# Where softmax and memory sums are divided out in a two-layer attention and Fourier kernel: through DRAM, or with 32x32 block transposes on VectorE

## The chip, the cores and the metric

The kernel runs on one core of a Trainium2 chip. The core has five engines that each work through their own list of instructions in the order written, and meet at semaphores: TensorE (PE; its weight loads are shown apart as PEld), VectorE (DVE), ScalarE (ACT), GpSimd (POOL) and SyncE (SP). SP computes nothing here; it issues every DMA, from one queue. Matmuls write to PSUM, eight tiles of 128x512 fp32; everything else is in SBUF or DRAM.

The metric is the device time of one execution in microseconds, as the median of several runs.

## What is computed

Two layers, each an attention with a compressive memory followed by a Fourier mixing. Cut to what matters:

```
S, D, H, Dh, N = 2048, 512, 32, 16, 4;  L = S // N          # four segments of 512 tokens
def A(x):                                                    # attention, segment by segment
    q, k, v = heads(x @ wq), heads(x @ wk), heads(x @ wv)
    g = sigmoid(beta);  M = 0;  z = 0                        # one gate for each head
    for s in range(N):
        a_dot = softmax(q[s] @ k[s].T * Dh**-0.5 + causal_mask) @ v[s]
        a_mem = (phi(q[s]) @ M) / (phi(q[s]) @ z + 1e-6)
        out[s] = g * a_mem + (1 - g) * a_dot
        M += phi(k[s]).T @ v[s];  z += sum(phi(k[s]))
    return out @ wo
def B(x):                                                    # real part of a 2-D DFT
    return Cr @ (x @ Wr.T) - Ci @ (x @ Wi.T)
for layer in range(2):
    x = x + A(layernorm(x))
    x = x + B(layernorm(x))
```

Both a_dot and a_mem are quotients: for every head and token a sum of weighted values over a sum of weights.

## The kernel before

**Units and tiles.** The 32 heads are four groups of eight, and a group is four pairs of heads. A unit `i` is one group in one segment of one layer, so there are 2 x 4 x 4 = 32 units. The value tile `vt` holds, for each pair, 16 value columns of the first head, 16 columns of ones, and 16 value columns of the second head. A matmul with 32 of these columns gives the weighted values of a head and its sum in one go: the two results of a unit, `e` and `o`, are PSUM tiles with tokens along the 512 columns, and in each block of 32 partitions (one head pair) 16 rows of values and 16 equal rows with the sum, values first in `e`, sum first in `o`. The same holds for the memory (`macc` in place of `vt`).

**The merge** (`t_merge`) makes one tile `n` out of `e` and `o`: values of the first heads from `e`, of the second heads from `o`, each divided by its sum and multiplied by its gate. It runs 56 times: 32 times for the softmax part (`gi` = 1, called by `s_m`), and 24 times for the memory part (`gi` = 0, called by `s_mem`; the first segment of a layer has no memory). ACT copies `e` and `o` whole to SBUF (`d`), makes the first half of `n` with a gate factor (`gm`) that is zero on the second heads' rows, and DVE adds the second half. Then four steps pass through DRAM, since a sum has to reach 16 partitions: one row of sums for each head is stored (`den`, two DMAs), loaded again with 128 partitions of 32 numbers (`dc`), inverted by DVE, stored (`rec`), and loaded with each row repeated over 16 partitions (`z`). One multiply on DVE or POOL ends the merge. `s_m` then adds the memory part and splits the result into two fp16 halves `ot`, which the output projection (`s_o`) takes once four units of a segment are done.

**What sets the order.** There are no loops over hardware iterations: the program is written out by a planner (`Plan`). Every part of the work is a Python generator that yields an engine, the tiles that it reads and the buffers that it wants; at each step the planner takes the part that can start first by its own model of the engines' times, and the instruction is appended to its engine's list. So a part with other operations, other costs or fewer waits changes the order of everything after it, on all engines. `tt` puts an elementwise operation of two tensors on DVE or POOL, whichever its model says ends it first. Buffers come from pools with a cap for each kind: all of `md`, `mz`, `en` and `ot` are kinds of 52 SBUF tiles `w`, `av`, `pj`, `ss` and `dft` kinds of the eight PSUM tiles `b`. The profile names tiles by these pool names, so most tiles read `w` or `b`; all instructions have the line of the helper `call` (L249).

**What else runs.** The attention's score matmuls run twice: `s_x` with queries along partitions, where DVE finds the row maxima (`t_max`: `junk` and `mx`), and `s_st` with keys along partitions, where ACT takes the exponential and POOL cuts the triangle (`t_sel`). `s_av` multiplies with `vt`. `s_c` prepares the DFT matrix for the first layer: a maximum over each block (`cam`, on DVE), a scale from it by way of PE, and a split into fp16 halves by ACT and POOL. `s_f` runs the DFT matmuls, `t_y` adds their results.

Of the kernel before, what the change touches and what calls it, by code (L numbers as in the profile page):

```python
# [8 lines left out]
F32 = mybir.dt.float32  # L9
# [3 lines left out]
AF = mybir.ActivationFunctionType  # L13
# [242 lines left out]
def body(ctx: ExitStack, tc: tile.TileContext, x, wq, wk, wv, wo, beta, wd, cs, out):  # L256
# [31 lines left out]
        xi0.append(xi)  # L288
    wsrc = [w.rearrange("(t p) n -> p t n", p=128) for w in (wq, wk, wv)]
    stage = [[y[:, 4 * n + g, :].rearrange("p (t n) -> p t n", t=KT) for n in range(3)] for g in range(NG)]  # L290
    gb = const.tile([128, 2, NG], F32, name="gb")

    def load(g, n):
        Y.dma_start(stage[g][n], wsrc[n][:, :, 128 * g:128 * g + 128])
# [17 lines left out]
    V.tensor_scalar(identf, jp, 0.0, None, op0=OP.is_equal)  # L312
    cmask = const.tile([128, 512], BF16, name="cmask")
    bd = const.tile([128, 2, 4, 32], F32, name="bd")
    gm = const.tile([128, 2, 2, NG], F32, name="gm")
    m0, m1, rp, ra = (const.tile([128, 1], F32, name=n) for n in ("m0", "m1", "rp", "ra"))
    done = set()
    ywritten = set()
    uses = {}
# [6 lines left out]
    def need(eng, *reads, tag=(), mode="m"):  # L326
        return eng, reads, (tag,) if isinstance(tag, str) else tag, mode
# [72 lines left out]
    def s_w():  # L400
        def part(n, g, how):
            i = 2 * g + n if n < 2 else 8
            yield need("A", tag="wv" if n == 2 else "wt")
            w = sb("wv" if n == 2 else "wt", F16, (128, 2, KT, 128))
            yield from how(w, stage[g][n], scl[:, i:i + 1])
            yield need("Y", w)
            Y.dma_start(wqkv[g][n], w)
            wnow[n, g] = w
            done.add(("W", n, g))

        def factors(g):
            for f, n, e in ((f_q, 0, -10), (f_k, 1, -10), (f_k2, 1, 12)):
                V.tensor_scalar(f[g], inv[:, 2 * g + n:2 * g + n + 1], 2.0 ** e, None, op0=OP.mult)
            V.tensor_scalar(f_s[g], inv[:, 2 * g:2 * g + 1], inv[:, 2 * g + 1:2 * g + 2], 2.0 ** 22,
                            op0=OP.mult, op1=OP.mult)

        for g in range(2):
            for n in range(2):
                yield need("V", stage[g][n])
                absmax(2 * g + n, flat(stage[g][n]))  # L420
        yield from scales(0, 4)
        for n in range(2):
            yield from part(n, 0, split)
        factors(0)
        factors(1)
        for n in range(2):
            yield from part(n, 1, split2)
        yield gate(*[("L", 0, t) for t in range(TT)])
        for g in range(NG):
            load(g, 2)  # L430
        for g in range(2, NG):
            for n in range(2):
                load(g, n)
        Y.dma_start(gb[:, 0, :], beta)
        for g in range(NG):
            yield need("V", stage[g][2])
            V.tensor_reduce(vm[:, g:g + 1], flat(stage[g][2]), axis=AX.X, op=OP.max, apply_absolute_value=True)
        V.tensor_reduce(amax[:, 8:9], vm, axis=AX.X, op=OP.max)
        for g in range(2, NG):
            for n in range(2):  # L440
                yield need("V", stage[g][n])
                absmax(2 * g + n, flat(stage[g][n]))
        yield from scales(4, 9)
        done.add("WL")
        factors(2)
        factors(3)
        for x in ((2, 0), (0, 2), (1, 2), (2, 1), (2, 2), (0, 3), (1, 3), (2, 3)):
            yield from part(*x, split2)
# [28 lines left out]
    def s_k():  # L477
        def bits(f, mask, scale):
            t = work.tile([128, 1], I32, name="bits", bufs=2)
            V.tensor_scalar(t, pi, mask, None, op0=OP.bitwise_and)  # L480
            V.tensor_copy(f, t)
            V.tensor_scalar(f, f, scale, None, op0=OP.mult)

        for i in range(NR):
            for t, c in ((qst[i], 0.0), (kst[i], K8192)):
                for a in range(2):
                    r = slice(64 * a + 32, 64 * a + 64)
                    yield need("G")
                    G.memset(t[r].rearrange("r p n -> r (p n)").bitcast(F32), c)
            done.add(("QI", i))  # L490
            done.add(("KI", i))
            if i == 0:
                yield need("V")
                V.memset(cmask[:, :384], 0.0)
                V.tensor_scalar(cmask[:, 384:], jp, 0.0, NEG, op0=OP.is_gt, op1=OP.mult)
                done.add("CM")
                yield gate(*[("L", 0, t) for t in range(TT)])
                for j in range(NR):
                    V.memset(vt[j][:, :, :, 1, :], 1.0)
                done.add("VI")  # L500
        yield need("V")
        bits(m1, 16, 1.0 / 16)
        V.tensor_scalar(m0, m1, -1.0, 1.0, op0=OP.mult, op1=OP.add)
        bits(rp, 3, 1.0)
        bits(ra, 64, 1.0 / 64)
        cj = sb("en", F32, (128, 2, 4, 32))
        G.iota(cj, pattern=[[0, 2], [1, 4], [0, 32]], base=0, channel_multiplier=0,
               allow_small_or_imprecise_dtypes=True)
        ca = sb("pn", F32, (128, 2, 4, 32))
        G.iota(ca, pattern=[[1, 2], [0, 4], [0, 32]], base=0, channel_multiplier=0,  # L510
               allow_small_or_imprecise_dtypes=True)
        yield need("V", cj, ca)
        V.tensor_scalar(cj, cj, rp, None, op0=OP.is_equal)
        V.tensor_scalar(ca, ca, ra, None, op0=OP.is_equal)
        V.tensor_tensor(bd, cj, ca, op=OP.mult)
        pl.close(cj, ca)
        yield gate("WL")
        yield need("A", gb)
        A.activation(gb[:, 1, :], gb[:, 0, :], AF.Exp, scale=1.0)
        A.activation(gb[:, 0, :], gb[:, 0, :], AF.Exp, scale=-1.0)  # L520
        yield need("V", gb)
        V.tensor_scalar(gb, gb, 1.0, None, op0=OP.add)
        V.reciprocal(gb, gb)
        for i in range(2):
            for j, m in enumerate((m0, m1)):
                V.tensor_scalar(gm[:, i, j, :], gb[:, i, :], m, None, op0=OP.mult)
        done.add("GM")

    def t_ln(src, xi, dst, key):
# [43 lines left out]

    def t_merge(e, o, gi, g, n, key):
        yield gate("GM")
        yield need("A", e, o, gm, tag=("md", "md"))
        ds = []
        for src in (e, o):
            d = sb("md")
            A.activation(d, src, AF.Copy)  # L580
            ds.append(d)
        A.activation(n, e, AF.Copy, scale=gm[:, gi, 0, g:g + 1])
        yield need("V", n)
        V.scalar_tensor_tensor(n, o, gm[:, gi, 1, g:g + 1], n, op0=OP.mult, op1=OP.add)
        pl.close(e, o)
        yield need("Y", *ds)
        den = tc.dram_tile([NP, 2, 512], F32)
        rec = tc.dram_tile([NP, 2, 512], F32)
        for a, d in enumerate(ds):
            Y.dma_start(den[:, a, :], d[16 - 16 * a:128:32, :], est=(530, 500))  # L590
        pl.close(*ds)
        yield need("Y", den)
        c = rg("dc", 3, F32, (128, 32))
        Y.dma_start(c, den.rearrange("p a (x c) -> (p a x) c", c=32), est=(350, 750))
        yield need("V", c)
        if not gi:
            V.tensor_scalar(c, c, 1e-6, None, op0=OP.add)
        V.reciprocal(c, c)
        yield need("Y", c)
        Y.dma_start(rec.rearrange("p a (x c) -> (p a x) c", c=32), c, est=(380, 450))  # L600
        yield need("Y", rec, tag="mz")
        z = sb("mz")
        Y.dma_start(z, rec.rearrange("p a n -> (p a) n").unsqueeze(1).to_broadcast([2 * NP, 16, 512]),
                    est=(650, 2100))
        yield need("VG", n, z)
        tt(n, n, z, OP.mult)
        pl.close(z)
        done.add(key)

    def t_split(p, key, f, kphi):  # L610
# [292 lines left out]
    def s_m():  # L903
        for i in range(NGRP):
            q, g = divmod(i, NG)
            s = q % NSEG
            yield gate(("E", i))
            yield need("A", tag=("en", "ot"))
            o1 = sb("en")
            ot = ots[i] = sb("ot", F16, (128, 2, 512))  # L910
            yield from t_merge(avs[i, 0], avs[i, 1], 1, g, o1, ("o1", i))
            if s:
                yield gate(("o2", i))
                yield need("VG", o1, o2s[i])
                tt(o1, o1, o2s[i], OP.add)
                pl.close(o2s[i])
            yield need("A", o1)
            A.activation(ot[:, 0], o1, AF.Copy, scale=32.0)
            yield need("V", ot)
            V.scalar_tensor_tensor(ot[:, 1], o1, 32.0, ot[:, 0], op0=OP.mult, op1=OP.subtract)  # L920
            pl.close(o1)
            done.add(("M", i))
# [297 lines left out]
```

## Time and profile before

| | |
|---|---|
| median of 3 runs | 1768.02 us (1767.25 to 1774.84) |
| the profiled execution | 1769.47 us |
| its span, from the first to the last instruction | 1767.7 us |
| mean granted clock of PE | 0.979 |
| packets moved by DMA | 240981, 242.41 MB |

A row of a group reads: line, engine, operation, out<-in, shapes, count, then busy us and mean ns of one, then the idle time of the engine just before these instructions with what ended it. `DVE junk L249 <- PE b L249: 65.4, 55, 5.1` in a list of waits means that DVE, before instructions that write `junk`, was idle for 65.4 us in all, 55 times, 5.1 us at the longest, until PE had written `b`. Idle time of an engine counts only where another engine, in the end PE, waits for it. "SPq" is SP's queue: its waits are in the issuing of DMAs.

### The profile page before, as it was taken

The page shows a single profiled execution, that of the slowest core. Times are in us where ns is not written, and L with a number is a line of the kernel's source. Part 1 is how long each engine was busy: PE and PEld are TensorE (multiplying, and loading weights), DVE is VectorE, ACT ScalarE, POOL GpSimd, SP SyncE. Part 2 cuts the span into 40 slices and gives each one's busy share as a digit, 9 for nine tenths or more (in the row PEclk, how much of TensorE's full clock was granted, in tenths as well). Part 3 has the DMA queues.
Part 4 walks back from the last instruction along what each step waited for, and adds up shares of the span by engine and source line. Part 5 has one row for each costly group of instructions (what it writes and reads, how often), then busy time and mean ns, then how long its engine had stood idle before and what let it go on. Part 6 is the DMA issues. An engine that isn't in the chain of part 4 may idle for free. (4 is left out here: it accounts for less than half of the span.)

```text
span 1767.7 us, 32331 instructions
## 1 busy us (share of the span) xinstructions
PE 1669.0 (94%) x11020; PEld 746.7 (42%) x11020; DVE 1090.7 (62%) x3392; ACT 898.9 (51%) x1521; POOL 740.5 (42%) x1118
## 2 busy tenths in 40 slices
PE   4988799999999999999899999999999999999999
PEld 2533334444444434444444443444444443444444
DVE  7787666496757775555587776645656765343222
ACT  3667757745755667345437755465564345410000
POOL 6446536554634555334435543443543433230000
PEclk8988899999999999999999999999999999999999
DMA  7565526564574534345875762454436342237103
GB/s 204 149 182 130 150 66 161 158 167 116 155 205 117 152 106 129 119 141 178 239 206 180 189 188 72 108 135 119 115 95 155 105 134 64 66 100 256 36 0 137
DMA packets 240981, 242.41 MB, mean 137 GB/s; under 512 B 129776, under 2 KB 152304, under 8 KB 240816
## 3 DMA queue, kind: packets, MB, share of 16 engines
q1 hardware_dynamic: 240816, 240.35, 49.0%
q8 instruction: 87, 1.43, 0.3%
q14 instruction: 78, 0.64, 0.1%
HBM read 152.96 MB, written 63.70 MB: 123 GB/s over the span
## 5 line engine op out<-in xcount | busy, mean ns | idle before, releaser
L249 PEld LDWEIGHTS <-w 128*128 128x128 f16 x4992 | 467.2, 98 | 610.0 <-issue 92.9
L249 PE MATMUL b<-w,w 128*128 128x512 f16 x3072 | 708.8, 381 | 6.4 <-POOL w L249 3.9
L249 POOL TENSOR_TENSOR w<-w,w 128x512 f16<-128x512 f32 (+1 forms) x314 | 379.0, 1211 | 421.9 <-ACT w L249 258.1
L249 DVE CUSTOM_DVE_ANT_0 junk<-b,cmask 128x256 bf16<-128x256 f32 (+3 forms) x1024 | 437.1, 483 | 66.0 <-PE b L249 65.4
L249 ACT ACTIVATE w<-b,fac 128x512 f32<-128x512 f32 x664 | 407.4, 696 | 128.7 <-PE b L249 125.8
L249 POOL TENSOR_SCALAR_AFFINE_SELECT w<-w 128x256 f32<-128x256 f32 (+1 forms) x640 | 229.5, 371 | 255.3 <-ACT w L249 245.1
L249 DVE SCALAR_TENSOR_TENSOR y<-b,fyu,y 128x512 f32<-128x512 f32 x232 | 173.5, 748 | 226.1 <-PE b L249 225.4
L249 ACT ACTIVATE w<-b 128x512 f16<-128x512 f32 (+1 forms) x240 | 137.1, 598 | 247.4 <-PE b L249 244.7
L249 ACT ACTIVATE w<-w,csc 128x512 f16<-128x512 f32 (+1 forms) x256 | 181.3, 721 | 80.2 <-DVE csc L249 63.3
L249 PE MATMUL b<-g,w 128*128 128x512 f16 x768 | 184.3, 383 | 5.4 <-DMA g<-w 2.6
L249 PE MATMUL b<-wd,w 128*128 128x512 f16 x768 | 180.3, 382 | 1.2 <-DMA w<-w 1.2
L249 ACT ACTIVATE w<-w 128x512 f16<-128x512 f32 (+1 forms) x144 | 90.8, 633 | 172.2 <-DVE w L249 129.7
L249 PE MATMUL b<-w,vt 128*32 128x512 f32 (+3 forms) x2048 | 174.1, 455 | 0.8 <-ACT w L249 0.5
L249 DVE SCALAR_TENSOR_TENSOR w<-b,w 128x512 f16<-128x512 f32 x128 | 87.7, 685 | 106.9 <-ACT w L249 106.7
L249 PE MATMUL b<-qst,kst 64*128 64x512 f16 (+3 forms) x1024 | 123.3, 307 | 17.1 <-ACT w L249 5.7
L249 PE MATMUL b<-kst,qst 62*128 62x256 f16 (+3 forms) x1024 | 121.1, 306 | 19.3 <-DVE mx L249 9.1
L249 PE MATMUL b<-w,g 128*128 128x128 f16 x1536 | 99.3, 223 | 5.6 <-ACT w L249 2.4
L249 PEld LDWEIGHTS <-g 128*128 128x128 f16 x1536 | 91.6, 100 | 21.8 <-issue 15.1
L249 PEld LDWEIGHTS b<-w,vt 128*32 128x32 f32 x2048 | 60.2, 111 | 91.3 <-issue 58.9
L249 PEld LDWEIGHTS <-kst 64*128 64x128 f16 x1024 | 39.8, 94 | 122.0 <-issue 107.6
L249 DVE TENSOR_REDUCE cam<-w 128x1 f32<-128x512 f32 x128 | 81.8, 675 | 12.9 <-DMA w<-in_cs_dram 12.6
L249 PE MATMUL b<-wo,w 128*128 128x512 f16 x384 | 86.0, 379 | 0.3 <-DVE y L249 0.3
(103 smaller groups left out, 912.4 us busy)
## 6 DMA issues: line engine op xcount, KB each, us to landing
w<-in_cs_dram SPq DMA_DIRECT2D x128, 256.0 KB
cc<-w SPq DMA_DIRECT2D x128, 256.0 KB
w<-cc SPq DMA_DIRECT2D x128, 256.0 KB
w<-w SPq DMA_DIRECT2D x96, 256.0 KB
d<-w SPq DMA_DIRECT2D x128, 128.0 KB
w<-rec SPq DMA_DIRECT2D x56, 256.0 KB
w<-in_x_dram SPq DMA_DIRECT2D x32, 256.0 KB
qst<-d SPq DMA_DIRECT2D x64, 128.0 KB
```

The source lines that it names most:

```text
L249: r = f(*args, **kw)
```

## The change

`t_merge` no longer goes through DRAM. DVE transposes `e` and `o` in blocks of 32x32 out of PSUM into two SBUF tiles `t` (kind `md`). A block holds 32 partitions of one head pair and 32 tokens; after the transpose the tokens lie along partitions, and the 32 rows of the pair along columns. So a token's sum stands in the same partition as its 16 values. DVE takes one column of sums out of each of the 16 blocks, scales it by the inverse of the gate (`gb`; for the memory part it adds 1e-6 first), both heads' into one tile `dn` of 32 columns, inverts `dn`, and two multiplies (DVE or POOL, by `tt`) write the 16 value columns of each block times its inverse sum into `n`. `n` stays transposed; the memory part is added in that form, and only then `s_m` transposes the sum back on DVE, into a buffer of the kind `mz`, ahead of the split into `ot`. `gb` gets a new layout, [128, part, head of the pair, group], with one load; the masks `m0`, `m1` and the masked gates `gm` go.

```
-    gb = const.tile([128, 2, NG], F32, name="gb")
+    gb = const.tile([128, 2, 2, NG], F32, name="gb")
...
-    gm = const.tile([128, 2, 2, NG], F32, name="gm")
-    m0, m1, rp, ra = (const.tile([128, 1], F32, name=n) for n in ("m0", "m1", "rp", "ra"))
+    rp, ra = (const.tile([128, 1], F32, name=n) for n in ("rp", "ra"))
...
-        V.reciprocal(gb, gb)
-        for i in range(2):
-            for j, m in enumerate((m0, m1)):
-                V.tensor_scalar(gm[:, i, j, :], gb[:, i, :], m, None, op0=OP.mult)
...
     def t_merge(e, o, gi, g, n, key):
         yield gate("GM")
-        yield need("A", e, o, gm, tag=("md", "md"))
-        ds = []
-        for src in (e, o):
-            d = sb("md")
-            A.activation(d, src, AF.Copy)
-            ds.append(d)
-        A.activation(n, e, AF.Copy, scale=gm[:, gi, 0, g:g + 1])
-        yield need("V", n)
-        V.scalar_tensor_tensor(n, o, gm[:, gi, 1, g:g + 1], n, op0=OP.mult, op1=OP.add)
-        pl.close(e, o)
-        yield need("Y", *ds)
-        den = tc.dram_tile([NP, 2, 512], F32)
-        rec = tc.dram_tile([NP, 2, 512], F32)
-        for a, d in enumerate(ds):
-            Y.dma_start(den[:, a, :], d[16 - 16 * a:128:32, :], est=(530, 500))
-        pl.close(*ds)
-        yield need("Y", den)
-        c = rg("dc", 3, F32, (128, 32))
-        Y.dma_start(c, den.rearrange("p a (x c) -> (p a x) c", c=32), est=(350, 750))
-        yield need("V", c)
-        if not gi:
-            V.tensor_scalar(c, c, 1e-6, None, op0=OP.add)
-        V.reciprocal(c, c)
-        yield need("Y", c)
-        Y.dma_start(rec.rearrange("p a (x c) -> (p a x) c", c=32), c, est=(380, 450))
-        yield need("Y", rec, tag="mz")
-        z = sb("mz")
-        Y.dma_start(z, rec.rearrange("p a n -> (p a) n").unsqueeze(1).to_broadcast([2 * NP, 16, 512]),
-                    est=(650, 2100))
-        yield need("VG", n, z)
-        tt(n, n, z, OP.mult)
-        pl.close(z)
+        ts = []
+        yield need("V", e, gb, tag=("md", "md"))
+        for p in (e, o):
+            t = sb("md")
+            ts.append(t)
+        for p, t in ((e, ts[0]), (o, ts[1])):
+            yield need("V", p)
+            V.transpose(t, p)
+            pl.close(p)
+        dn = rg("dn", 4, F32, (128, 2, 16))
+        for a, t in enumerate(ts):
+            den = t.rearrange("p (b j) -> p b j", j=32)[:, :, 16 - 16 * a]
+            f = gb[:, gi, a, g:g + 1]
+            if gi:
+                V.tensor_scalar(dn[:, a], den, f, None, op0=OP.mult)
+            else:
+                V.tensor_scalar(dn[:, a], den, 1e-6, f, op0=OP.add, op1=OP.mult)
+        V.reciprocal(dn, dn)
+        for a, t in enumerate(ts):
+            yield need("VG", t, dn)
+            r = slice(16 * a, 16 * a + 16)
+            tt(n.rearrange("p (b j) -> p b j", j=32)[:, :, r], t.rearrange("p (b j) -> p b j", j=32)[:, :, r],
+               dn[:, a].unsqueeze(2).to_broadcast([128, 16, 16]), OP.mult)
+            pl.close(t)
         done.add(key)
...
     def s_m():
...
-            yield need("A", tag=("en", "ot"))
+            yield need("V", tag=("en", "ot"))
...
+            yield need("V", o1, tag="mz")
+            ob = sb("mz")
+            V.transpose(ob, o1)
+            pl.close(o1)
+            o1 = ob
             yield need("A", o1)
             A.activation(ot[:, 0], o1, AF.Copy, scale=32.0)
```

The planner then writes another order. In the rows below, `ISA junk,mx` is one maximum of `t_max` and the `ISA mx` behind it the reading of its result; `w` and `b` are SBUF and PSUM tiles with their running numbers, which differ between the two programs.

The first place is DVE's list where the tenth batch of DFT blocks has its maxima taken (`cam`; in the profile before, some 495 to 503 us after the start). Before:

```order
L249 ISA junk,mx<-b_6935,cmask 128x512
L249 ISA mx 128x1
L249 TENSOR_REDUCE cam<-w_6401 128x1
L249 RECIPROCAL dc<-dc 128x32
L249 SCALAR_TENSOR_TENSOR w_6980<-b_6939,w_6980 128x512
L249 TENSOR_REDUCE cam<-w_6518 128x1
L249 TENSOR_SCALAR w_6940<-b_6939,fac 128x512
L249 TENSOR_REDUCE cam<-w_6581 128x1
L249 SCALAR_TENSOR_TENSOR w_7015<-b_6974,w_7015 128x512
L249 TENSOR_REDUCE cam<-w_6711 128x1
```

And with the change:

```order
L249 ISA junk,mx<-b_6806,cmask 128x512
L249 ISA mx 128x1
L249 STREAM_TRANSPOSE w_6857<-b_6590 128x512
L249 STREAM_TRANSPOSE w_6858<-b_6597 128x512
L249 TENSOR_SCALAR dn<-w_6857,gb 128x16
L249 TENSOR_SCALAR dn<-w_6858,gb 128x16
L249 RECIPROCAL dn<-dn 128x32
L249 TENSOR_REDUCE cam<-w_6325 128x1
L249 TENSOR_REDUCE cam<-w_6369 128x1
L249 TENSOR_REDUCE cam<-w_6427 128x1
L249 TENSOR_REDUCE cam<-w_6652 128x1
L249 SCALAR_TENSOR_TENSOR w_6899<-b_6863,w_6899 128x512
```

Before, a reciprocal that needs a load from DRAM stands between the first and the second of four maxima. Now a merge's transposes, scalings and reciprocal stand as one piece ahead of all four.

The second place is SP's list of DMAs at the same stage. Before:

```order
L249 DMA den<-w_6893 4x512
L249 DMA den<-w_6895 4x512
L249 DMA w_6944<-in_cs_dram 128x512
L249 DMA cc_182<-w_6907 128x1024
L249 DMA dc<-den 128x32
L249 DMA rec<-dc 128x32
L249 DMA w_6970<-w_136 128x1024
L249 DMA w_6972<-w_137 128x1024
L249 DMA w_6984<-rec 128x1x512
L249 DMA rec<-dc 128x32
```

And with the change:

```order
L249 DMA w_6868<-in_cs_dram 128x512
L249 DMA cc_179<-w_6837 128x1024
L249 DMA w_6893<-w_134 128x1024
L249 DMA d<-w_6899 64x2x512 x2
L249 DMA w_6923<-w_132 128x1024
L249 DMA w_6925<-w_135 128x1024
L249 DMA w_6927<-w_136 128x1024
L249 DMA w_6956<-w_137 128x1024
```

The stores and loads of `den`, `dc` and `rec` are gone; weights (`w_6970<-w_136`), blocks of the DFT matrix (`in_cs_dram`, `cc`) and projections (`d`) follow each other without them.

More of the change, by code (lines that the diff above doesn't have):

```diff
@@ L433, in s_w @@
                 load(g, n)
-        Y.dma_start(gb[:, 0, :], beta)
+        Y.dma_start(gb[:, 0].rearrange("p a g -> p (a g)"), beta)
         for g in range(NG):
@@ L501, in s_k @@
         yield need("V")
-        bits(m1, 16, 1.0 / 16)
-        V.tensor_scalar(m0, m1, -1.0, 1.0, op0=OP.mult, op1=OP.add)
         bits(rp, 3, 1.0)
@@ L518, in s_k @@
         yield need("A", gb)
-        A.activation(gb[:, 1, :], gb[:, 0, :], AF.Exp, scale=1.0)
-        A.activation(gb[:, 0, :], gb[:, 0, :], AF.Exp, scale=-1.0)
+        A.activation(gb[:, 1], gb[:, 0], AF.Exp, scale=1.0)
+        A.activation(gb[:, 0], gb[:, 0], AF.Exp, scale=-1.0)
         yield need("V", gb)
         V.tensor_scalar(gb, gb, 1.0, None, op0=OP.add)
-        V.reciprocal(gb, gb)
-        for i in range(2):
-            for j, m in enumerate((m0, m1)):
-                V.tensor_scalar(gm[:, i, j, :], gb[:, i, :], m, None, op0=OP.mult)
         done.add("GM")
@@ L1201 @@
         "wo": f["A_wo"],
-        "beta": _np.repeat(f["A_beta"], DH).reshape(NG, 128).T,
+        "beta": _np.repeat(f["A_beta"].reshape(NG, NP, 2).transpose(1, 2, 0).reshape(NP, 2 * NG), 32, axis=0),
         "wd": _np.concatenate([f["B_dft_hid_re"].T, f["B_dft_hid_im"].T], axis=1),
```

## The prediction

> **What bounds the kernel now.** I read the page's head first, then busy time in stretches of the span, then what TensorE (PE) waits for, and only then the engines that the change touches.
>
> ```profile
> span 1767.7 us, 32331 instructions
> PE 1669.0 (94%) x11020; PEld 746.7 (42%) x11020; DVE 1090.7 (62%) x3392; ACT 898.9 (51%) x1521; POOL 740.5 (42%) x1118
> 150.00:200.00 50.00, 38.07 (x315) 18.91 (x314) 31.39 (x116) 38.93 (x66) 28.64 (x39) 0.84 0.42 117
> 200.00:250.00 50.00, 46.19 (x278) 16.87 (x277) 39.82 (x153) 27.61 (x49) 21.13 (x40) 0.88 0.34 95
> 1500.00:1600.00 100.00, 100.00 (x549) 43.83 (x548) 38.51 (x72) 27.11 (x47) 25.62 (x37) 1.00 0.36 106
> 1600.00:1700.00 100.00, 100.00 (x465) 45.36 (x464) 29.17 (x39) 1.19 (x2) 0.00 (x0) 1.00 0.29 96
> ```
>
> In the stretches the columns are length, then the busy time of PE, PEld, DVE, ACT and POOL, then the granted clock of PE. PE is busy for 1669.0 of 1767.7 us. The change touches no matmul, so the time can move only through the 98.7 us in which PE idles, and through the clock, which is 0.84 and 0.88 in the two early stretches and 1.00 later. From 1500 to 1700 us PE has no idle time: nothing that the last merges do there can show. What PE waits for in the rest:
>
> ```profile
> PE b L249 <- ACT w L249: 19.7, 43, 2.4
> PE b L249 <- DVE mx L249: 18.9, 35, 1.4
> PE b L249 <- DVE amax L249: 17.4, 2, 13.6
> PE b L249 <- DVE cam L249: 8.3, 6, 4.4
> PE b L249 <- POOL w L249: 5.8, 5, 1.9
> ```
>
> The columns are total us, times, longest. The amax wait lies in the opening, before any merge, and stays. No wait on a merge is in the list. What PE waits for is ACT emptying score tiles and DVE finishing the row maxima (mx) and the block maxima of the DFT matrix (cam), in many waits of about half a microsecond. So the question is what the change does to the queues of DVE, ACT and POOL, which work in the order written.
>
> Those queues do stand still for the merges:
>
> ```profile
> POOL w L249 <- DMA w<-rec: 66.8, 17, 13.9
> DVE dc L249 <- DMA dc<-den: 36.6, 25, 3.7
> DVE w L249 <- DMA w<-rec: 16.2, 4, 5.4
> 499.02 0.35 DVE L249 RECIPROCAL dc<-dc 128x32 f32<-128x32 f32 x1 [2.66 <-DMA dc<-den]
> 503.00 0.39 PE L249 MATMUL b<-cam,ones 128*128 128x4 f32 x2 [1.92 <-DVE cam L249]
> 627.42 0.18 DVE L249 TENSOR_SCALAR dc<-dc 128x32 f32<-128x32 f32 x1 [2.04 <-DMA dc<-den]
> 630.43 0.28 PE L249 MATMUL b<-identf,mx 128*32 128x128 f32 x1 [1.30 <-DVE mx L249]
> ```
>
> The last four rows are instructions in order of time (start, length, and in brackets the idle time before them and what ended it). At 499.02 DVE had stood 2.66 us for the load of dc, with three cam reductions queued behind it; four microseconds later PE stood 1.92 us for the last of these. At 627.42 it stood 2.04 us, with row maxima behind it, and PE then stood 1.30 us for mx. That is how a merge reaches PE today: not by its result, but by holding DVE.
>
> **The change, part by part.** Prices come from these rows:
>
> ```profile
> L249 ACT ACTIVATE w<-b 128x512 f32<-128x512 f32 x112 | 60.7, 597 | 51.2 <-PE b L249 49.3 <-DMA qst<-mhl 1.8
> L249 ACT ACTIVATE w<-b,gm 128x512 f32<-128x512 f32 x56 | 39.1, 698 | 0.0
> L249 DVE SCALAR_TENSOR_TENSOR w<-b,gm,w 128x512 f32<-128x512 f32 x56 | 41.9, 747 | 21.6 <-ACT w L249 21.5
> L249 DVE RECIPROCAL dc<-dc 128x32 f32<-128x32 f32 x56 | 19.6, 350 | 12.0 <-DMA dc<-den 11.0
> L249 DVE TENSOR_SCALAR dc<-dc 128x32 f32<-128x32 f32 x24 | 8.3, 346 | 25.6 <-DMA dc<-den 25.6
> L249 DVE CUSTOM_DVE_ANT_0 junk<-b,cmask 128x512 bf16<-128x512 f32 x256 | 163.5, 683 | 22.9 <-PE b L249 22.7
> L249 DVE TENSOR_SCALAR w<-w,fac 128x512 f32<-128x512 f32 x24 | 13.3, 552 | 43.6 <-ACT w L249 43.6
> L249 DVE RECIPROCAL gb<-gb 128x8 f32<-128x8 f32 x1 | 0.2, 203 | 0.0
> L249 POOL TENSOR_TENSOR macc<-macc,w 128x256 f32<-128x256 f32 x14 | 10.5, 749 | 18.3 <-DVE w L249 16.7 <-PE b L249 1.7
> L249 POOL TENSOR_TENSOR w<-w,w 128x512 f32<-128x512 f32 x122 | 155.9, 1280 | 204.6 <-ACT w L249 68.1 <-DMA w<-rec 66.8 <-DVE mx L249 26.0
> ```
>
> *ACT* loses three activations for each of 56 merges: 60.7 + 39.1 = 99.8 us, 11% of its 898.9. Nothing is added to it.
>
> *DVE* loses 41.9 + 19.6 + 8.3 = 69.8 us. It gains 112 block transposes out of PSUM, 32 back in SBUF, 112 small scalings over 16 columns and 56 reciprocals over 32 columns. The trace has no transpose on DVE. Lower bound: the 552 ns of a 512-wide SBUF scaling. Upper bound: from the reciprocals (350 ns for 32 columns, 203 for 8) a slow element costs (350 - 203)/24 = 6.1 ns, so 512 would take 203 + 504 x 6.1 = 3.3 us. I take 683 ns from PSUM, as the 512-wide pass over scores does, which also reads one PSUM tile, and 620 ns in SBUF, between that and 552. So 112 x 0.683 + 32 x 0.62 = 96 us; the reciprocals stay at 19.6; the scalings at 0.2 us (the 8-column instruction takes 203 ns) make 22. Added 138, removed 70: +68 us of work. Against that the stalls of 36.6 + 16.2 = 52.8 us go. DVE is tied up for 1090.7 + 52.8 = 1143.5 us before and 1159 after: +1%, nearly even.
>
> [...] No run here shows a transpose yet.
>
> *POOL*: where one 512-wide product stood (1280 ns), there are now two of 16x16 elements against a broadcast factor; 256-wide products take 749 ns. The program as ordered has 110 of these on POOL and 2 on DVE, and 53 fewer wide products there: 110 x 0.749 - 53 x 1.28 = +15 us. The broken rows of 16 may cost more; up to twice 749, which is 82 us further, on an engine with 42% load. The 66.8 us of standing still for rec go.
>
> *SP's queue and the transfers*:
>
> ```profile
> SPq L249 <- DVE dc L249: 64.6, 35, 3.7
> SPq L249 <- DMA den<-w: 48.6, 51, 3.1
> SPq L249 <- DMA rec<-dc: 29.7, 36, 2.3
> L249 SPq DMA_DIRECT2D den<-w x112: 483/520/607, 86.8 to 1536.4; - x112
> L249 SPq DMA_DIRECT2D dc<-den x56: 319/326/1545, 89.2 to 1538.2; - x56
> L249 SPq DMA_DIRECT2D rec<-dc x56: 319/326/789, 96.0 to 1540.8; - x56
> L249 SPq DMA_DIRECT2D w<-rec x56: 618/649/674, 106.3 to 1542.2; - x56
> ```
>
> 280 issues go: 112 x 0.520 + 112 x 0.326 + 56 x 0.649 = 131 us of issuing, and 64.6 + 48.6 + 29.7 = 143 us in which SP stood for a merge with weight, input and score loads behind it. PE waits for hardly any load itself, so I value this at zero. If that is wrong it is a gain of a few us.
>
> *The merge's own length*: the two rows below are the last merge of layer 0, from its first copy out of PSUM to the multiply that ends it (two multiplies merged in the second row).
>
> ```profile
> 707.03 1.09 ACT L249 ACTIVATE w<-b 128x512 f32<-128x512 f32 x2 [0.81 <-PE b L249]
> 718.33 2.61 POOL L249 TENSOR_TENSOR w<-w,w 128x512 f32<-128x512 f32 x2 [10.87 <-DMA w<-rec]
> ```
>
> It takes 718.33 - 707.03 + 1.3 = 12.6 us. The new chain is 2 x 0.683 + 2 x 0.2 + 0.35 + 2 x 0.749 + 0.62 = 4.2 us. Segments can close 8 us earlier, but PE had DFT work to fill that time, so I count nothing for it.
>
> **The sum**, in PE idle time. (a) DVE no longer stands for dc and rec: in the two places shown 4.7 us of stall cost PE 3.2. Over all 52.8 us that ratio would be 36, more than PE's whole wait for mx and cam (27.2). Bounds 3.2 and 27.2. I take 10, nearer the lower end, since most stalls meet a PE with other work. (b) POOL no longer stands: at most the 5.8 us that PE waits for POOL; I take 2. (c) ACT 11% lighter: 11% of 19.7 is 2.2, at most a third, 7; I take 2. (d) DVE's new work comes in lumps of 2.1 us (two transposes, two scalings, a reciprocal) in front of row maxima, where lumps of 1.1 us stood (0.747 + 0.350): 56 us more in lumps; at the share of a tenth to a third that would be 6 to 19 us, but most fall where DVE used to stand, so I take +3. Sum: -10 - 2 - 2 + 3 = -11 us. The profiled execution took 1769.47 us (span 1767.7 and 1.8 around it), which gives 1758.5; the median of the runs is 1.45 us lower, which gives 1757.
>
> **The rivals.** *Even* (1765): the lumps of (d) stand where the stalls stood, and PE waits for mx as before. For: DVE is tied up as long as before. Against: a lump begins when PE is done, a stall when a transfer lands, and the written order knows the first better. (a) shrinks to 3 and (d) grows to 4; with (b) and (c) that is -3. A change of less than 0.5% cannot be told from none in this kernel's measurement.
>
> *The clock* (1743): filled gaps before 250 us also bring the granted clock back. At 0.84 and 0.88, 50 x 0.16 + 50 x 0.12 = 14 us are lost in two stretches; all of it on top of -11 gives 1743. Against: those gaps are mostly ACT and mx waits that remain. [...]
>
> *DVE stands for PE* (1783), the other side: the first copy of a merge carries the wait for the last value matmul. ACT carries it now, 49.3 us over the copies; a transpose takes it onto DVE, with row maxima queued behind. If all 49.3 us arrive there, on top of 68 us more work and less 52.8 of stalls, DVE is tied up 64 us longer; at a conversion into PE idle time of 0.3 (between the 10 of 52.8 that (a) takes and the 0.68 of the two places shown) that is +19, and with (b) and (c) alone as gains the time is 1768 + 19 - 4 = 1783. It decides from about 53 us of DVE idle time ended by PE in front of transposes.
>
> [...]
>
> **How the numbers follow.** My forecast gets 0.37, its own range 1748 to 1759; the clock 0.08; even 0.31; DVE standing for PE 0.17; slow transposes 0.07. Faster by over 0.5% (below 1759.2) is 0.45, within 0.31, slower (above 1776.9) 0.24. The range of 1738 to 1786 runs from below the clock case to beyond the first slower one.
>
> **What would show it.** Right: no DVE or POOL idle time ended by a DMA of a merge; STREAM_TRANSPOSE near 0.68 us; ACT near 800 us; DVE near 1159; PE's waits for mx and cam together under 20 us. Wrong: DVE idle before transposes ended by PE above 50 us; mx waits above 30 us; transposes over 1 us; a later granted clock below 1.00. A PE idle sum of 98.7 us or more would refute the forecast whatever the parts do.

## The result

The change makes the kernel faster: 1723.61 us in the median (1722.0 to 1727.48, 5 runs) against 1769.79 us before on the same chip (1767.25 to 1774.84, 5 runs). The ratio is 0.9744, with a 95% interval of 0.9719 to 0.977. That is 46 us where 11 were forecast, and outside the range of 1738 to 1786.

The head of the page after the change, and four of its stretches (length, then busy time of PE, PEld, DVE, ACT and POOL, then PE's clock):

```profile
span 1725.7 us, 31875 instructions
PE 1650.1 (96%) x11020; PEld 741.4 (43%) x11020; DVE 1136.4 (66%) x3557; ACT 813.0 (47%) x1353; POOL 740.9 (43%) x1176
150.00:200.00 50.00, 40.05 (x316) 19.40 (x309) 39.80 (x142) 37.69 (x62) 30.81 (x42) 0.80 0.49 140
200.00:250.00 50.00, 47.57 (x326) 18.59 (x324) 36.63 (x131) 29.95 (x52) 24.07 (x49) 1.00 0.27 68
1000.00:1100.00 100.00, 97.77 (x746) 44.79 (x745) 73.15 (x249) 46.92 (x82) 41.60 (x75) 1.00 0.47 130
1100.00:1200.00 100.00, 100.00 (x754) 43.92 (x752) 64.44 (x229) 55.72 (x96) 47.35 (x88) 1.00 0.44 113
```

The span fell by 42.0 us. PE's idle time fell from 98.7 to 75.6 us, by 23.1. But PE's busy time fell too, from 1669.0 to 1650.1, by 18.9, with the same 11020 matmuls. In the two early stretches the clock now loses 50 x 0.20 = 10 us where it lost 14, so the clock is a small part of this; its mean over the span went from 0.979 to 0.981. Which matmuls shrank is in the groups, before:

```profile
L249 PE MATMUL b<-w,vt 128*32 128x512 f32 (+3 forms) x2048 | 174.1, 455 | 0.8 <-ACT w L249 0.5
L249 PE MATMUL b<-qst,kst 64*128 64x512 f16 (+3 forms) x1024 | 123.3, 307 | 17.1 <-ACT w L249 5.7
L249 PE MATMUL b<-kst,qst 62*128 62x256 f16 (+3 forms) x1024 | 121.1, 306 | 19.3 <-DVE mx L249 9.1
```

and after:

```profile
L249 PE MATMUL b<-w,vt 128*32 128x512 f32 (+3 forms) x2048 | 167.8, 451 | 0.7 <-POOL w L249 0.6
L249 PE MATMUL b<-kst,qst 62*128 62x256 f16 (+3 forms) x1024 | 116.1, 305 | 13.5 <-DVE mx L249 5.7
L249 PE MATMUL b<-qst,kst 64*128 64x512 f16 (+3 forms) x1024 | 114.4, 306 | 5.4 <-ACT w L249 2.3
```

These are the value matmuls and the two passes of scores. Their busy time fell by 6.3 + 8.9 + 5.0 = 20.2 us and the idle time before them by 0.1 + 11.7 + 5.8 = 17.6 us: 38 of the 42 us of span. The mean length of one hardly changed (455 to 451 ns, 307 to 306, 306 to 305). Several of them run beside each other: 1024 x 0.307 = 314 us of matmuls lie in 123.3 us of busy time. So when they lie closer together, the busy time falls with the same work. A busy PE was no floor here. What had kept them apart is not shown; x9 below has the order of before and none of the transfers; added up shape by shape, where matmuls of two shapes that overlap count twice, these three groups take 474.0 us in it, against 479.2 before and 457.9 after, so most of this fall came with the new order.

What PE waits for after the change:

```profile
PE b L249 <- DVE amax L249: 15.8, 2, 13.6
PE b L249 <- DVE mx L249: 10.6, 18, 2.2
PE b L249 <- ACT w L249: 8.9, 22, 2.4
PE b L249 <- DVE cam L249: 7.2, 8, 2.5
PE b L249 <- POOL w L249: 6.6, 6, 2.1
```

mx and cam together fell from 27.2 to 17.8 us, ACT from 19.7 to 8.9, and POOL rose from 5.8 to 6.6. The new operations, by their groups:

```profile
L249 DVE STREAM_TRANSPOSE w<-b 128x512 f32<-128x512 f32 x112 | 73.6, 693 | 14.3 <-PE b L249 14.3
L249 DVE STREAM_TRANSPOSE w<-w 128x512 f32<-128x512 f32 x32 | 22.5, 702 | 3.4 <-POOL w L249 3.4
L249 DVE TENSOR_SCALAR dn<-w,gb 128x16 f32<-128x16 f32 x112 | 25.6, 269 | 0.0
L249 POOL TENSOR_TENSOR w<-w,dn 128x256 f32<-128x256 f32 x110 | 67.6, 635 | 153.6 <-DVE dn L249 112.8 <-DVE mx L249 10.0 <-DVE mhl L249 9.8
```

A transpose out of PSUM takes 693 ns, one in SBUF 702. DVE stands 14.3 us for PE in front of transposes. POOL now stands 112.8 us for DVE's inverse sums, more than the 66.8 us that it stood for rec; with 43% load it can.

### The profile page after: what moved, and what is told of

Its sections match the earlier page's. It is cut to its first block, busy times and chain, and to the rows that moved or that the text cites. A ratio compares the mean times of both kernels' runs of the same rounds, so it can differ in the third digit from the quotient of the medians.

```text
span 1725.7 us, 31875 instructions
## 1 busy us (share of the span) xinstructions
PE 1650.1 (96%) x11020; PEld 741.4 (43%) x11020; DVE 1136.4 (66%) x3557; ACT 813.0 (47%) x1353; POOL 740.9 (43%) x1176
## 4 chain that ended last, share of the span: by engine, by line
PE 75%; DVE 8%; ACT 5%; DMA 5%; issue 3%; POOL 2%; SPq 1%; ACTq 0%; POOLq 0%; DVEq 0%
PE b L249 75%; ACT w L249 4%; DVE junk L249 2%; DVE w L249 2%; DMA w<-in_cs_dram 2%; POOL w L249 1%; SPq L249 1%; DMA w<-w 1%; DVE y L249 1%; DVE cam L249 1%; DMA w<-x 1%; DMA w<-in_x_dram 1%; DVE bst L249 0%; DVE mx L249 0%; DMA y<-in_wv_dram 0%
## 5 line engine op out<-in xcount | busy, mean ns | idle before, releaser
L249 POOL TENSOR_TENSOR w<-w,w 128x512 f16<-128x512 f32 (+1 forms) x261 | 310.7, 1196 | 216.9 <-ACT w L249 206.2
L249 ACT ACTIVATE w<-b 128x512 f16<-128x512 f32 x128 | 76.4, 597 | 202.7 <-PE b L249 200.1
L249 PE MATMUL b<-w,vt 128*32 128x512 f32 (+3 forms) x2048 | 167.8, 451 | 0.7 <-POOL w L249 0.6
L249 POOL TENSOR_TENSOR w<-w,dn 128x256 f32<-128x256 f32 x110 | 67.6, 635 | 153.6 <-DVE dn L249 112.8
L249 PE MATMUL b<-kst,qst 62*128 62x256 f16 (+3 forms) x1024 | 116.1, 305 | 13.5 <-DVE mx L249 5.7
L249 PE MATMUL b<-qst,kst 64*128 64x512 f16 (+3 forms) x1024 | 114.4, 306 | 5.4 <-ACT w L249 2.3
```

Source lines behind the costliest of these rows:

```text
L249: r = f(*args, **kw)
```

## The experiments

All times below are medians, all ratios against the kernel before, measured beside it on the same chip. The median of the kernel before lay between 1765 and 1770 us on these chips, so a difference in us between runs on two chips is uncertain by a few us. Theory *ACT*: score tiles in PSUM are emptied sooner because ACT lost 100 us of work. Theory *stalls*: DVE and POOL no longer stand for transfers. Theory *queue*: SP and the transfers themselves are out of the way of all other loads. Theory *order*: the planner wrote a better order of the lists.

**ACT relieved in the kernel before** (x1):

```
-        for src in (e, o):
-            d = sb("md")
-            A.activation(d, src, AF.Copy)
...
-            Y.dma_start(den[:, a, :], d[16 - 16 * a:128:32, :], est=(530, 500))
+            Y.dma_start(den[:, a, :], n[16 - 16 * a:128:32, :], est=(530, 500))
...
-        if not gi:
-            V.tensor_scalar(c, c, 1e-6, None, op0=OP.add)
+        V.tensor_scalar(c, c, 0.0, 4096.0, op0=OP.mult, op1=OP.add)
```

> The kernel before, without the two whole copies of each merge on ACT (112 x 0.6 us); the row sums sent through DRAM come from n instead, and what is inverted is a constant, so the outputs are not the reference's. All four transfers and the waits on them stay. Theory ACT (the gain of the change comes from ACT having 100 us less to do, so that it empties score tiles sooner): 60 of those 100 us are taken away, so about 0.6 of the gain of 46 us, near 1742. Theory stalls (the gain comes from DVE and POOL no longer standing for transfers): no change, 1769 within 9 us. Theory queue (SP and the transfers themselves): no change either.

1768.52 us, ratio 0.9993 (0.9977 to 1.0008). Nothing is gained. ACT is busy for 846.6 us where it was 898.9, and PE waits 18.7 us for it where it waited 19.7. While the transfers stay, ACT's copies cost nothing that shows. This is weaker than it looks: the order is another one too, DVE has 32 more small operations, and x11 below shows that an order alone can cost 17 us.

**ACT loaded again in the changed kernel** (x2):

```
+        yield need("A", e, o, gb)
+        for _ in range(3):
+            A.activation(scr, cmask, AF.Copy)
         yield need("V", e, gb, tag=("md", "md"))
```

> The changed kernel with three extra 512-wide ACT activations in front of each merge, from a constant into a scratch tile that nobody reads (168 x some 0.6 us, about what the change took from ACT). Theory ACT: the gain goes, near 1769. Theories stalls and queue: 1724 within 9 us.

1733.33 us, ratio 0.9804 (0.9777 to 0.9832): 10 us slower than the changed kernel, at the edge of what the other theories allowed and far from 1769, with ACT at 909.1 us, more than before the change. The order is another one here too, and x8 below shows that this alone can move it as much. ACT is not where most of the gain is from.

**SP loaded again in the changed kernel** (x3). The five DMAs of a merge come back as a task of their own that nobody reads; the kind `mz` may hold two buffers in place of one:

```
+    def t_dram(ts):
+        yield need("Y", *ts)
...
+        Y.dma_start(c, den.rearrange("p a (x c) -> (p a x) c", c=32), est=(350, 750))
+        yield need("Y", c)
+        Y.dma_start(rec.rearrange("p a (x c) -> (p a x) c", c=32), c, est=(380, 450))
+        yield need("Y", rec, tag="mz")
+        z = sb("mz")
+        Y.dma_start(z, rec.rearrange("p a n -> (p a) n").unsqueeze(1).to_broadcast([2 * NP, 16, 512]),
+                    est=(650, 2100))
+        pl.close(z)
...
             V.transpose(t, p)
             pl.close(p)
+        spawn(t_dram(ts))
```

> The changed kernel with the five DMAs of each merge (den twice, dc, rec, rec broadcast) issued again on SP with their waits on each other, moving constants, and with no engine waiting for them. Theory queue: most of the gain goes, 1755 to 1769. Theories ACT and stalls: 1724 within 9 us.

1781.72 us, ratio 1.0066 (1.004 to 1.0093). All of the gain is gone, and more, though no engine reads what is moved.

**The kernel before with later readers** (x4):

```
-        Y.dma_start(c, den.rearrange("p a (x c) -> (p a x) c", c=32), est=(350, 750))
+        Y.dma_start(c, den.rearrange("p a (x c) -> (p a x) c", c=32), est=(350, 4750))
...
-                    est=(650, 2100))
+                    est=(650, 8100))
```

> The kernel before, where the planner's model of the two loads of a merge is 4 and 6 us longer (dc and the broadcast rec), so that their readers on DVE and POOL are written later in the lists and stand less; the same instructions otherwise. Theory stalls: a good part of the gain, 1735 to 1755. Theories ACT and queue: 1769 within 9 us. If the order alone scatters the time, it could be off by 10 to 20 us either way with none of these.

1763.04 us, ratio 0.997 (0.9953 to 0.9987): 5 us better, less than the theory asked for and within what an order alone moves. Yet the standing did go down, on DVE from 36.6 us to almost nothing and on POOL from 66.8 to half:

```profile
DVE dc L249 <- DMA dc<-den: 0.9, 1, 0.9
POOL w L249 <- DMA w<-rec: 32.8, 6, 11.1
```

SP's standing for a merge did not: 63.3 + 47.3 + 41.5 = 152 us, against 143. So less standing on DVE and POOL did not bring the gain by itself in this order. Since the order differs, it is not a measurement of either part.

x3 mixes two things: SP is busy, and the planner writes another order because it reckons with that. The next runs take them apart: x5 keeps the lists of x3 row for row, x6 and x7 those of the changed kernel.

**The order of x3 without its DMAs** (x5). `Ghost` lets the planner count a DMA and issues nothing; all five go through it (the last two lines against x3):

```
+class Ghost(Eng):
+    def __getattr__(self, name):
+        def call(*args, **kw):
+            self.plan.dma = kw.pop("est", None)
+            self.plan.op(self.key, name, args, kw)
+        return call
...
+    Z = Ghost(None, "Y", pl)
...
-        Y.dma_start(c, den.rearrange("p a (x c) -> (p a x) c", c=32), est=(350, 750))
+        Z.dma_start(c, den.rearrange("p a (x c) -> (p a x) c", c=32), est=(350, 750))
```

> The changed kernel in the order of x3 on all engines: the planner reckons with the five DMAs of each merge, but they are not issued. Theory order (the gain of the change comes from the planner finding SP free and writing a better order for PE): as x3, 1782 within 9 us. Theory queue (the gain comes from SP really being free, whatever the order): near the changed kernel, 1724 to 1735.

1751.18 us, ratio 0.992 (0.9893 to 0.9946). Between the two theories: in one and the same order the DMAs cost 1.0066 - 0.992 = 1.5%, some 26 us, and the order of x3 is by itself about 28 us worse than that of the changed kernel.

**The order of the changed kernel with the DMAs** (x6), in a chain as before the change, and unchained (x7). This is x6; in x7 the load of c and the broadcast read a constant in DRAM (`rfix`) and the store of rec reads `ones`:

```
+        sy = nc.sync
...
+        for a in range(2):
+            sy.dma_start(den[:, a, :].rearrange("p (x c) -> p x c", c=128),
+                         ones[16 - 16 * a:128:32, :].unsqueeze(1).to_broadcast([4, 4, 128]))
+        c = rg("dc", 3, F32, (128, 32))
+        sy.dma_start(c, den.rearrange("p a (x c) -> (p a x) c", c=32))
+        sy.dma_start(rec.rearrange("p a (x c) -> (p a x) c", c=32), c)
+        sy.dma_start(zz, rec.rearrange("p a n -> (p a) n").unsqueeze(1).to_broadcast([2 * NP, 16, 512]))
         dn = rg("dn", 4, F32, (128, 2, 16))
```

> The changed kernel in its own order on PE, DVE, ACT and POOL, with the five DMAs of each merge put into SP's list behind the transposes, each waiting for the one before it as before the change; the planner doesn't know of them, and nobody reads what they move (the broadcast goes to DRAM). Theory queue: 1760 to 1785. Theory order: 1724 within 9 us.

> As x6, but the five DMAs don't wait for each other (they read constants), so SP only spends the time of issuing them, 131 us in all, and the traffic is the same. If within theory queue it is SP's standing for one DMA's end before the next that costs: 1724 to 1740, well below x6. If it is the issuing or the traffic: as x6.

x6: 1855.02 us, ratio 1.0499 (1.0468 to 1.053). x7: 1752.98 us, ratio 0.9917 (0.9889 to 0.9945). x6 is above what was expected of either theory, and x7 lies between its two. So in the order of the changed kernel the unchained DMAs cost 29 us, and their standing for each other on SP another 102. The waits of SP's queue in x6 that belong to the chain, with those of PE and its weight loads that were small before:

```profile
SPq L586 <- DMA den<-ones: 104.2, 57, 3.7
SPq L587 <- DMA dc<-den: 77.8, 56, 2.5
SPq L588 <- DMA rec<-dc: 64.7, 56, 2.5
```

```profile
PE b L249 <- DMA qst<-mhl: 26.5, 10, 8.1
PE b L249 <- DMA w<-w: 20.9, 7, 8.3
...
PEld L249 <- DMA qst<-mhl: 37.8, 20, 8.4
...
PEld L249 <- DMA w<-w: 28.6, 10, 8.8
```

SP stands 104.2 + 77.8 + 64.7 = 247 us for one DMA of a merge before it may issue the next, and the row maxima (mhl into qst) and the transposed and weight tiles (w) behind it come late: here PE does wait for loads. In the kernel before, the same chain stood for 143 us, but the planner had written other DMAs between its steps, and PE hardly waited for these loads:

```profile
PE b L249 <- DMA w<-w: 2.9, 4, 1.2
PE b L249 <- DMA qst<-mhl: 2.5, 3, 1.3
```

What that order cost in exchange, x6 does not show.

**Another order only**: one constant of the planner in the changed kernel (x8, and x15 the other way, with 140.0) and in the kernel before (x11):

```
-    LAT = dict(T=197.0, V=150.0, A=165.0, G=100.0, Y=0.0)
+    LAT = dict(T=197.0, V=160.0, A=165.0, G=100.0, Y=0.0)
```

> The changed kernel with one constant of the planner's model moved (DVE's latency 160 in place of 150 ns), which reorders the lists and changes no instruction. It measures how far an order that is merely another one moves the time: 1724 within 5 us if little, 10 to 20 us off if the order alone scatters much.

> The kernel before with the one constant of the planner's model that x8 moves in the changed kernel (DVE's latency 160 in place of 150 ns). It measures how far merely another order moves the time of before: 1760 to 1785 if as in x8.

> The changed kernel with the planner's DVE latency at 140 in place of 150 ns: a third order of the same instructions. With x8 it says whether 1724 is a usual or a lucky order: 1730 to 1745 if lucky, 1724 within 5 us if usual.

x8: 1737.4 us, ratio 0.9832 (0.9809 to 0.9855). x11: 1781.88 us, ratio 1.009 (1.0064 to 1.0116). x15: 1732.63 us, ratio 0.9797 (0.9777 to 0.9817). An order alone moves either kernel by 9 to 17 us. 1724 is the best of three, and by the expectation of x15 a lucky order. The order of before was the better one of its two as well. At the constant of 160 the change gives 0.9832 / 1.009 = 0.974, worked out from two ratios, the same as at 150. So the gain does not hang on one lucky pair.

**The order of the kernel before, without the DMAs** (x9), **and with them unread** (x10). The lists of PE and ACT are those of before, row for row, and DVE and POOL do the same operations on a constant in place of dc and z:

```
-        V.reciprocal(c, c)
+        twin(V, "reciprocal", (c, c), (c, c if not gi else ones[:, 0:32]))
...
-        tt(n, n, z, OP.mult)
+        twin(E, "tensor_tensor", (n, n, z), (n3, n3, ones.unsqueeze(1).to_broadcast([128, 4, 128])), op=OP.mult)
```

(`twin` issues the second list of operands and tells the planner the first; this is x9, which also sends the five DMAs to `Ghost`; in x10 the inverse goes into a tile of its own, from which rec is stored.)

> The kernel before in its own order on all engines, without the five DMAs of each merge; inverse sums come from a constant instead of DRAM (scaled by 1/4096), so the outputs are not the reference's, and every engine does the same work. SP is relieved and DVE and POOL have no transfer of a merge to stand for. What the transfers cost in the order of before: if it is the whole gain of the change, 1723 within 5 us; if the order has a share in it as the two orders in x5 and the changed kernel suggest, 1735 to 1745.

> As x9, but the five DMAs are issued and wait for each other and for DVE as before; only that nobody reads what they bring, so DVE and POOL don't stand for them. Theory stalls: what x9 gains over before is gained here too. Theory queue: nothing is gained, 1769 within 9 us.

x10: 1748.03 us, ratio 0.9903 (0.9882 to 0.9923). x9: 1732.84 us, ratio 0.982 (0.9797 to 0.9843). With DVE and POOL no longer standing, 1.0% is gained; with SP, the memory path and the tiles that the transfers hold free as well, another 0.8%. Both theories hold, with about equal parts when they are taken away in this sequence; the other sequence was not run. PE's part of the page, x10 first:

```profile
PE 1663.6 (95%) x11020; PEld 745.5 (43%) x11020; DVE 1088.6 (62%) x3392; ACT 897.4 (51%) x1521; POOL 737.1 (42%) x1118
PE 1658.6 (96%) x11020; PEld 744.3 (43%) x11020; DVE 1092.8 (63%) x3392; ACT 897.1 (52%) x1521; POOL 738.3 (43%) x1118
```

The spans are 1748.0 and 1730.0 us, so PE idles for 84.4 and 71.4 us, against 98.7 before, and its busy time falls a little too. SP's waits in x10 and x9 go with the second part:

```profile
SPq L249 <- POOL w L249: 318.5, 145, 14.7
...
SPq L249 <- DMA den<-w: 46.3, 48, 3.7
SPq L606 <- DVE dc L334: 45.9, 27, 3.4
...
SPq L249 <- DMA rec<-dc: 32.7, 36, 2.8
```

```profile
SPq L249 <- POOL w L249: 447.9, 150, 15.2
SPq L249 <- DVE y L249: 127.2, 29, 83.3
SPq L249 <- PE b L249: 118.4, 84, 14.2
```

In x10, the first fence, SP stands for 46.3 + 45.9 + 32.7 = 125 us for a merge. In x9 it doesn't, and it stands longer for data that POOL has yet to make (447.9 us for 318.5). So its other loads can go out sooner. Who gains by that is in the lists of waits: added up over all loads, DVE stands 43.8 us for a DMA in x10 and 25.6 in x9, POOL 74.6 and 66.7, PE itself only 6.0 and 4.4. No engine reads what a merge's transfers bring in either run. PE's waits for DVE, POOL and ACT fall by 6.6, 2.2 and 3.1 us, which is most of the 13 us of its idle time. That the one comes from the other fits the rows; it was not followed wait by wait.

**Issuing or bytes**: x7 with DMAs of 128 bytes in place of the five (x12, below, five times for each merge), with the broadcast alone (x13), with the four small ones alone (x14):

```
+            nc.sync.dma_start(tiny, ones[i:i + 1, 0:32])
```

> As x7, but each of the five DMAs moves only 128 bytes from a constant to DRAM: SP still has 280 more to issue, and next to no traffic is added. If the 29 us of x7 are the time of issuing on SP, 1745 to 1753; if they are the traffic, 1724 to 1730.

> As x7, with only the broadcast of each merge (one DMA of 256 KB; 56 issues of 0.68 us, 38 us in all). If the 29 us of x7 are bytes moved, nearly all of it: 1745 to 1753. If they are SP's issuing time (38 of 149 us), 1728 to 1735.

> As x7, with only the four small DMAs of each merge (den twice, dc, rec; 224 issues, 111 us in all, 48 KB for each merge). If the 29 us of x7 are SP's issuing time, 1742 to 1750; if they are bytes moved, 1724 to 1732.

x12: 1728.4 us, ratio 0.9793 (0.9767 to 0.9818). x13: 1730.46 us, ratio 0.9786 (0.9766 to 0.9805). x14: 1732.46 us, ratio 0.9804 (0.9788 to 0.982). Over the changed kernel that is 5, 7 and 9 us (9, 7 and 11 by the ratios), against 29 for all five together in x7. SP's times of issuing in x7, and in x12 the last row:

```profile
L585 SPq DMA_DIRECT2D den<-ones x112: 508/557/623, 82.6 to 1517.5; - x112
L588 SPq DMA_DIRECT2D dc<-rfix x56: 320/434/1257, 83.8 to 1518.1; - x56
L589 SPq DMA_DIRECT2D rec<-ones x56: 326/430/1628, 84.3 to 1518.6; - x56
L590 SPq DMA_DIRECT2D zz<-rfix x56: 661/684/1522, 84.8 to 1519.0; - x56
```

```profile
L580 SPq DMA_DIRECT2D tiny<-ones x280: 214/250/1390, 82.0 to 1491.4; - x140
```

By the medians x7 issues for 112 x 0.557 + 56 x (0.434 + 0.430 + 0.684) = 149 us, and x12 for 70. By the medians of x7, the four small ones of x14 make 111 of the 149, the broadcasts of x13 38. Neither issuing nor bytes alone explains the 29: both halves cost little, and all five together cost nearly twice what the halves add up to (29 for 16). That would fit a queue with some slack, which the first half uses up; it is not shown beyond these four points.

No run beat the changed kernel.

## Why the prediction was wrong

**The direction and the mechanism of the stalls were right.** DVE and POOL held back PE by standing for a merge's transfers. Terms (a) and (b) put this at 12 us; x10 measures it alone, in one and the same order, at 1.0%, 17 us. In PE's own waits the terms came out unevenly. (a) and (d) together were near: mx and cam fell by 9.4 us, where 7 were forecast. (b) did not show: the wait for POOL rose by 0.8 us, where 2 less were forecast. (c) was too small: the wait for ACT fell by 10.8 us, where 2 were forecast; in x9, with ACT's work as before, it had already fallen by 7.4, so a lighter ACT is not the main reason.

**The step that failed** is in the paragraph on SP's queue: "PE waits for hardly any load itself, so I value this at zero." The 131 us of issuing and 143 us of standing were counted rightly, and then dropped because PE's list of waits held hardly any load. x9 against x10 measures them at 0.8%, about 15 us, in one and the same order on every engine; x6 and x7 measure the same transfers in the order of the changed kernel at 131 and 29 us. PE's own waits for loads were no measure of it: they came to 10.1 us before and 9.3 after. In x9 against x10 it is DVE and POOL that stand less for loads, by 18.2 and 7.9 us, and PE stands less for them.

**A second step failed with it:** the time "can move only through the 98.7 us in which PE idles, and through the clock". 18.9 of the 42.0 us of span came out of PE's busy time, in the score and value matmuls. In x9, in the order of before, 10.4 of 37.7 us did. So the whole of PE's named waits, which capped terms (a), (b) and (c), was no cap. The idle time itself fell by 23.1 us where 11 were forecast.

**The signs.** Most of those named for being right held: no engine stands for a DMA of a merge, the transposes are near 0.68 us, ACT is at 813 us, mx and cam together at 17.8. The time was 33 us below the forecast all the same, since none of them looked at SP.

**What is left** is the step from x9 to the changed kernel, 0.982 to 0.9744: 13 us by the ratios, 9 by the times. In it PE's busy time falls by 8.5 us and its idle time rises by 4.2. It holds what the engines do differently (ACT 84 us lighter, DVE 44 us heavier, a shorter merge) and a different order. Terms (c) and (d) put the engines at +1 us. x2 says that ACT's part can be up to 10 us, and x8 that an order can be worth 14, as much as this whole step; these runs don't part them. That stays open.

**Durations.** The transposes out of PSUM were right (693 ns for 683), those in SBUF 702 for 620: in the changed kernel both take about as long as the 512-wide pass over scores, 681 ns there. DVE gained 45.7 us of busy time where 68 were forecast: the new rows came to 96.1 + 25.6 us, and 19.7 for the reciprocals, as forecast, but the total came out some 26 us lower than these rows give. The list by shapes shows about 20 of it in other groups, among them: one kind of small scaling, writing cgm, fell from 19.0 to 13.2 us, and the six 512-wide products that DVE had (4.7 us) and the products for gm (3.3) are gone, which the forecast had not counted. The rest was not followed up. POOL's products took 635 ns for 749.

**The rivals.** *Even*: refuted; the lumps did not take the stalls' place, mx fell from 18.9 to 10.6 us. *The clock*: its 1743 us was nearer than the forecast, but not by its mechanism; the early stretches went from 0.84 and 0.88 to 0.80 and 1.00, 4 us in all. From 150 to 200 us PE idles less than before (10.0 us for 11.9) at a lower clock, so the amount of idle time alone does not set it; what does, no run here shows. Nor was the clock 1.00 everywhere later on: it was 0.97 from 400 to 500 us before and after. *DVE stands for PE*: it does, for 14.3 us, far from the 53 from which it would decide. *Slow transposes*, given 0.07: refuted; its sign was transposes over 1 us, and one took 693 ns.

## What to carry to other kernels

Where a planner or a hand-made order spreads work around a slow queue, the engine that bounds the kernel can show hardly any wait for that queue, as here (10.1 us for loads in a span of 1767.7), and its busy time is no floor either (it fell by 18.9 us with the same matmuls); the price is measured by taking the transfers out with the order kept, or putting them in. A chain of DMAs on one queue cost far more here than the same DMAs unchained, by what stood behind it: the five of a merge cost 131 us chained and 29 us unchained in one order. Before a gain of one or two per cent is read as a mechanism, the scatter of the order is worth a run: one constant moved this kernel by 9 to 17 us.

## What the runs showed of the hardware

A 32x32 block transpose of 128x512 fp32 on DVE takes 693 ns from PSUM and 702 ns from SBUF, about as long as the 512-wide maxima over scores (683 ns before, 681 after). A product of 16x16 elements in each partition against a factor of one number per 16 takes POOL 635 ns, less than a plain 256-wide addition there, which took 749 ns before and 725 after. The time that SP needs to issue a DMA differs with its form, by the medians: 250 ns for 128 bytes in x12, 323 to 326 ns for 128 rows of 128 bytes in x6 and before, 520 to 557 ns for a store into four rows of 2 KB (before, x6 and x7), 649 to 684 ns for the broadcast (the same three). Form is not all: in x7, where SP does not stand for the DMA before, the 128 rows take 430 and 434 ns.
